# Exp issued a step later than its top-k, its reciprocal two; feed-forward pieces counted out, some held back

## The chip, the cores and the metric

One core of a Trainium2 chip runs the whole program. It has a matrix engine (TensorE, PE in the rows; PEld is its weight load), a vector engine (VectorE, DVE), an activation engine (ScalarE, ACT), a general engine (GpSimd, POOL) and a queue that starts transfers (SyncE, SP). Each engine takes its instructions in the order in which the program lists them; where one waits for another engine's result, everything behind it on its engine waits too. The metric is the device time in microseconds (us), lower is better.

## What is computed

The first half is attention in which every query keeps only its 32 largest scores. q, k and v have 8 batches, 8 heads, 576 rows and 64 columns, all in fp32:

```
scores = (q @ k.T) / 8
kth    = 32nd largest score of each row
attn   = exp(scores - max) where scores >= kth, else 0
attn   = attn / (sum(attn) + 1e-9);  x = attn @ v
```

The heads of a row are laid side by side, which gives x with 4608 rows of 512. The second half is a feed-forward layer on x, with w_in of 512 x 2048 and w_out of 2048 x 512: h = x @ w_in, g = h * clip(h + 3, 0, 6) / 6, out = g @ w_out.

## The kernel before

The program is written out as one list of steps, and the order in that list is the order on every engine. The unit of attention work (class Unit) is one pair of heads with 128 query rows: two rows of 576 scores per partition. 576 is 4 x 128 + 64, so each head pair has a remainder of 64 rows; both heads of a remainder go into one half-size unit, a rest unit. There are 160 units, 20 to a batch: 16 full and 4 rest. In an even batch four full units (the four head pairs of one query tile) are followed by a rest unit, in an odd batch the rest unit comes first.

What a unit goes through, with the lines that issue it:

- scores (L198 to L220): matmuls into big, then ScalarE copies into sc. big is one PSUM tile of four banks with a single buffer; scores, the transposes of a unit and the transposes of a pair (L171) all use it in turn, so each must wait until ScalarE has copied out the one before.
- top(0) to top(3) (L228): per row a MAX8 (eight largest) and, but for the last round, a MATCH_REPLACE8 that takes them out. All on VectorE.
- exp (L240): three tiny GpSimd operations (kth L247, shift L248 and L249), then on ScalarE two Prelu (L251) and two Exp with a sum (L256), then den on GpSimd (L261).
- weights (L263): reciprocal on VectorE (L265) and two GpSimd multiplications (L267).
- transpose (L271): nine (rest: six) transposes on TensorE into big, copied by ScalarE to eT (L280).
- values (L282): matmuls of eT with v into pv, copied to xT (L410). Full units do this two at a time, after the second of the two.

When the four head pairs of a tile are done, a feed-forward is put on the list todo; there are 36 in all. It is a generator (feed_forward, L300) that yields 16 times, so it is handed out as 16 pieces: eight h pieces of eight matmuls each, then eight acc pieces of two matmuls each. After every second h piece comes a Relu on ScalarE (L317); the multiplication that closes the gate (L321, VectorE) is called two pieces later. piece(count) takes the next pieces from the front of todo, or nothing if it is empty.

The loop from L440 runs 162 steps. Step n issues top(0) to top(3) of unit n, scores of unit n + 1, and (from step 9 on) transposes and values of unit n - 2. In the first eight steps the weights of the feed-forward are also loaded and converted (convert_step, on ScalarE, VectorE and GpSimd), and the lag is one step.

Order in a step from 9 on: scores(n + 1); top(0); two pieces (one in a rest step); top(1); transpose(n - 2); top(2); one piece; weights(n - 1); transposes of the next batch's pair, in 4 of 20 steps; one more piece in a full step; values(n - 2); top(3); two pieces more in every fourth step; exp(n). After the loop the pieces that remain run alone.

Of the kernel before, what the change touches and what calls it, by code (L numbers as in the profile page):

```python
# [27 lines left out]
def kernel(  # L28
# [17 lines left out]
    NFC = FF // P  # L46
# [140 lines left out]
    class Unit:  # L187
# [94 lines left out]
        def values(self, dst):  # L282
            pr, eT = self.pair, self.eT
            for c in range(J + 1):
                for hh in range(2):
                    if self.rest:
                        rhs = eT[:, c if c < J else J + hh, hh * R : (hh + 1) * R]
                    else:
                        rhs = eT[:, c if hh == 0 or c == J else J + 1 + c, :]
                    nc.tensor.matmul(  # L290
                        dst[hh * D : (hh + 1) * D, :],
                        pr.vm[:, hh, c, :] if c < J else pr.vr[:, hh, :],
                        rhs,
                        start=(c == 0),
                        stop=(c == J),
                    )
# [3 lines left out]
    def feed_forward(xT, rows):  # L300

        gs = []
        for f0 in range(0, NFC, 4):
            h = ps_w.tile([P, 512], F32, tag="w", name="h")
            for f in range(f0, f0 + 4):
                if f == f0 + 2:
                    yield None
                for i in range(NHP):
                    nc.tensor.matmul(  # L309
                        h[:, (f - f0) * P : (f - f0 + 1) * P],  # L310
                        w_in[:, i, f * P : (f + 1) * P],
                        xT[:, i, :],
                        start=(i == 0),
                        stop=(i == NHP - 1),
                    )
            g = gpool.tile([P, 512], F32, tag="g", name="g")
            nc.scalar.activation(g[:], h[:], AF.Relu, bias=three[:], scale=1.0)  # L317
            gs.append(g)

            def gate(g=g, h=h):  # L320
                nc.vector.scalar_tensor_tensor(  # L321
                    out=g[:], in0=g[:], scalar=6.0, in1=h[:], op0=ALU.min, op1=ALU.mult
                )

            yield gate
        acc = ps_w.tile([P, DM], F32, tag="w", name="acc")
        for f in range(NFC):
            nc.tensor.matmul(  # L328
                acc[:],
                gs[f // 4][:, (f % 4) * P : (f % 4 + 1) * P],  # L330
                w_out[:, f, :],
                start=(f == 0),
                stop=(f == NFC - 1),
            )
            if f % 2 == 1:
                if f == NFC - 1:
                    o = opool.tile([P, DM], F32, tag="o", name="o")
                    nc.scalar.mul(o[:], acc[:], 1.0 / 6.0)  # L338
                    for p0, p1, dst in rows:
                        nc.sync.dma_start(dst, o[p0:p1, :])  # L340
                yield None
# [6 lines left out]
    units = []  # L348
    for b in range(B):
        for qt in range(J):  # L350
            full = [Unit(pairs[b, hp], qt) for hp in range(NHP)]
# [4 lines left out]
    NU = len(units)  # L356
    todo = []
    gates = []

    def piece(count=1):  # L360
        for _ in range(count):
            while todo:
                try:
                    gates.append(next(todo[0]))
                    break
                except StopIteration:
                    todo.pop(0)
            else:
                gates.append(None)
            if len(gates) > 2:  # L370
                gate = gates.pop(0)
                if gate:
                    gate()
# [4 lines left out]
    def convert_step(depth=1):  # L378

        if converting and (len(converting) > depth or not chunks):  # L380
            next(converting.pop(0), None)
        if chunks:
            c = convert(*chunks.pop(0))
            next(c)
            converting.append(c)

    EARLY = 8
    LAG = 2
    state = {}

    def values(n):

        u = units[n]
        b, hp = u.pair.b, u.pair.hp
        if u.rest:
            if b % 2 == 0 and hp == 0:
                state["xr"] = xrpool.tile([P, NHP, P], F32, tag="xr", name="xr")
            group, w = [u], R
            dst = state["xr"][:, hp : hp + 1, (b % 2) * R : (b % 2 + 1) * R]
        else:  # L400
            if hp % 2 == 0:
                return
            if hp == 1:
                state["xT"] = xtpool.tile([P, NHP, P], F32, tag="xT", name="xT")
            group, w = [units[n - 1], u], P
            dst = state["xT"][:, hp - 1 : hp + 1, :]
        pv = ps_w.tile([P, 512], F32, tag="w", name="pv")
        for i, v in reversed(list(enumerate(group))):
            v.values(pv[:, i * w : (i + 1) * w])
        nc.scalar.copy(dst, pv[:, 0 : len(group) * w].rearrange("p (u q) -> p u q", q=w))  # L410
        if hp == NHP - 1:
            if not u.rest:
                rows = [(0, P, out[b * S + u.qt : b * S + JP : J, :])]
                todo.append(feed_forward(state["xT"], rows))
            elif b % 2 == 1:
                rows = [
                    (i * R, (i + 1) * R, out[(b - 1 + i) * S + JP : (b + i) * S, :])
                    for i in range(2)
                ]
                todo.append(feed_forward(state["xr"], rows))  # L420

    def pair_at(n, first):

        b, at = divmod(n, per_batch)
        hp, odd = divmod(at - first, 3)
        return pairs[b + 1, hp] if b + 1 < B and not odd and 0 <= hp < NHP else None
# [13 lines left out]
    for n in range(NU + LAG):  # L440
        early = n < EARLY
        u = units[n] if n < NU else None
        full = not (u and u.rest)
        d = n - (1 if early else LAG)
        d = d if 0 <= d < NU and (early or d >= EARLY - 1) else None
        depth = 2 if n < 3 else 1
        if n + 1 < NU:
            units[n + 1].scores()
        if n < 2:
            pairs[0, n + 2].transpose()  # L450
        if n == 0:
            pairs[0, 3].load()
        if n in (1, 2):
            pairs[0, n + 1].load_values()
        if u:
            u.begin()
            u.top(0)
        p = pair_at(n, 6)
        if p:
            p.load()  # L460
            p.load_values()
        convert_step(depth)
        piece(2 if full else 1)
        if u:
            u.top(1)
        if d is not None:
            if not early:
                units[d].transpose()
        convert_step(depth)
        if u:  # L470
            u.top(2)
        piece()
        convert_step(depth)
        if 1 <= n < NU + 1:
            units[n - 1].weights()
        if d is not None and early:
            units[d].transpose()
            piece()
        p = pair_at(n, 8)
        if p:  # L480
            p.transpose()
        if full and not early:
            piece()
        if d is not None:
            values(d)
        if u:
            u.top(3)
        convert_step(depth)
        if n % 4 == 3 and n > 2 * EARLY:
            piece(2)  # L490
        if u:
            u.exp()
    while todo:
        piece()
    piece(2)
# [34 lines left out]
```

## Time and profile before

| | |
|---|---|
| median of 3 runs | 1875.74 us (1875.71 to 1878.25) |
| the profiled execution | 1877.58 us, its span 1875.8 us |
| PE busy | 1672.3 us, 89% of the span |
| PEld busy | 1228.7 us, 66% |
| DVE busy | 1550.3 us, 83% |
| ACT busy | 964.2 us, 51% |
| POOL busy | 409.0 us, 22% |
| mean granted TensorE clock | 0.951 |

The span goes from the first to the last instruction. Busy shares are averages over stretches with different limits, and a busy PE counts its slow stretches (half clock) as busy too. The rows below come from four views: busy times by stretch, waits, the chain that ended last, and the timeline. In a timeline row the first number is the start, the second the duration of the whole group (the ends of matmuls are modelled, so the start of the next PE row is the better end), and brackets hold idle time before it and what ended it.

### The profile page before, as it was taken

To read this page: it belongs to the slowest core of one execution; us is meant where nothing else is said; L and a number is where in the kernel's file an instruction comes from. 1 tells how busy PE (TensorE), PEld (TensorE's weight loads), DVE (VectorE), ACT (ScalarE), POOL (GpSimd) and SP (SyncE) were. 2 spreads that over 40 slices of the span, in tenths; PEclk is the share of its full clock that TensorE was granted. 3 is DMA by queue.
4 is the path that set the end of the run, shared out by engine and by line. 5 is a ranking of instruction groups with operands and counts; after the bars stand their busy time and mean duration, and the time that the engine had idled before them with its cause. 6 is when DMAs were issued, how large, how long until landed. Compare 5 with 4: busy or idle time off the path is not lost.

```text
span 1875.8 us, 30943 instructions
## 1 busy us (share of the span) xinstructions
PE 1672.3 (89%) x11872; PEld 1228.7 (66%) x11872; DVE 1550.3 (83%) x3249; ACT 964.2 (51%) x1717; POOL 409.0 (22%) x1038
## 2 busy tenths in 40 slices
PE   3366999888999999889999999898899999988899
PEld 2254776666777766567777766676776767666685
DVE  6877998889988887988989888887998887888950
ACT  4554555545545554555545545545555555445540
POOL 3553221122121111221112111211211121112210
PEclk9878999899999999899999999989999999989999
DMA  6441000110010100100001110101001110000000
GB/s 188 141 125 44 20 7 7 44 45 6 7 26 26 45 7 7 44 25 20 7 9 45 27 28 7 34 11 44 7 7 26 26 44 7 6 7 6 7 7 12
DMA packets 101140, 56.53 MB, mean 30 GB/s; under 512 B 84096, under 2 KB 92288, under 8 KB 100992
## 3 DMA queue, kind: packets, MB, share of 16 engines
q1 hardware_dynamic: 100992, 54.55, 10.6%
q8 instruction: 94, 1.54, 0.3%
q14 instruction: 54, 0.44, 0.1%
HBM read 45.09 MB, written 9.44 MB: 29 GB/s over the span
## 4 chain that ended last, share of the span: by engine, by line
PE 82%; ACT 10%; issue 3%; POOL 3%; DVE 1%; SPq 1%; DMA 1%; ACTq 0%
PE h L309 27%; PE acc L328 25%; PE pv L290 11%; PE big L278 9%; PE big L214 6%; ACT sc L256 3%; ACT eT L280 2%; ACT sc L251 2%; PE big L207 2%; PE big L179 2%; ACT sc L215 1%; POOL a L108 1%; POOL w_in L121 1%; ACT o L338 1%; POOL w_out L121 1%
## 5 line engine op out<-in xcount | busy, mean ns | idle before, releaser
L231 DVE MAX8 m<-wk 128x8 f32<-128x576 f32 x864 | 614.1, 748 | 2.1
L328 PE MATMUL acc<-w_out,g 128*128 128x512 f32 x1152 | 527.8, 600 | 0.3 <-DVE g L321 0.3
L309 PE MATMUL h<-xT,w_in 128*128 128x128 f32 x4096 | 490.9, 278 | 7.4 <-DVE y L117 7.4
L309 PEld LDWEIGHTS h<-xT,w_in 128*128 128x128 f32 x4096 | 470.4, 192 | 14.0 <-DVE y L117 7.8
L235 DVE MATCH_REPLACE8 wk<-m,wk 128x576 f32<-128x576 f32 x576 | 424.0, 743 | 0.0
L328 PEld LDWEIGHTS acc<-w_out,g 128*128 128x128 f32 x1152 | 207.3, 190 | 210.1 <-issue 202.4
L278 PE MATMUL big<-ident,sc 128*128 128x128 f32 x1344 | 189.8, 289 | 122.5 <-ACT sc L218 49.2
L267 POOL TENSOR_SCALAR sc<-sc,den 128x576 f32<-128x576 f32 x288 | 212.5, 747 | 368.3 <-DVE den L265 362.9
L278 PEld LDWEIGHTS big<-ident,sc 128*128 128x128 f32 x1344 | 163.2, 150 | 163.5 <-POOL den L261 78.4
L280 ACT COPY eT<-big 128x1152 f32<-128x1152 f32 (+1 forms) x160 | 169.1, 1057 | 183.3 <-PE big L278 183.3
L251 ACT ACTIVATE sc<-sc,kth 128x576 f32<-128x576 f32 x288 | 208.7, 769 | 34.3 <-POOL kth L247 34.3
L261 POOL TENSOR_SCALAR den<-den 128x2 f32<-128x2 f32 (+1 forms) x160 | 34.9, 218 | 868.1 <-ACT sc L256 868.1
L321 DVE SCALAR_TENSOR_TENSOR g<-g,h 128x512 f32<-128x512 f32 x144 | 97.7, 679 | 151.8 <-ACT g L317 151.8
L256 ACT ACTIVATE sc<-sc,shift 128x576 f32<-128x576 f32 x288 | 219.4, 763 | 3.3 <-ACT sc L251 0.4
L317 ACT ACTIVATE g<-h,three 128x512 f32<-128x512 f32 x144 | 99.0, 687 | 229.0 <-PE h L309 229.0
L231 DVE MAX8 m<-sc 128x8 f32<-128x576 f32 x288 | 204.0, 745 | 14.8 <-ACT sc L218 14.8
L235 DVE MATCH_REPLACE8 wk<-m,sc 128x576 f32<-128x576 f32 x288 | 212.0, 743 | 0.0
L290 PE MATMUL pv<-eT,vm 128*64 128x128 f32 (+1 forms) x2560 | 188.6, 298 | 25.4 <-ACT eT L280 25.4
L290 PEld LDWEIGHTS pv<-eT,vm 128*64 128x64 f32 x2560 | 157.1, 156 | 62.9 <-ACT eT L280 32.0
L214 PE MATMUL big<-kq 64*128 64x512 f32 (+1 forms) x1024 | 179.8, 472 | 20.1 <-ACT kq L185 11.7
L214 PEld LDWEIGHTS big<-kq 64*128 64x128 f32 x1024 | 94.5, 200 | 123.7 <-issue 87.9
L410 ACT COPY xT<-pv 128x256 f32<-128x256 f32 x64 | 23.8, 373 | 232.5 <-PE pv L290 232.5
(43 smaller groups left out, 1033.9 us busy)
## 6 DMA issues: line engine op xcount, KB each, us to landing
kin<-in_k_dram SPq DMA_DIRECT2D x64, 128.0 KB, 3.1
qin<-in_q_dram SPq DMA_DIRECT2D x64, 128.0 KB, 2.9
st<-in_moe_w_in_dram SPq DMA_DIRECT2D x16, 512.0 KB, 4.1
vm<-in_v_dram SPq DMA_DIRECT2D x64, 128.0 KB, 2.4
st<-in_moe_w_out_dram SPq DMA_DIRECT2D x16, 512.0 KB, 3.7
out_dram<-o SPq DMA_DIRECT2D x32, 256.0 KB, 2.2
rest<-in_k_dram SPq DMA_DIRECT2D x32, 32.0 KB, 2.6
rest<-in_q_dram SPq DMA_DIRECT2D x32, 32.0 KB, 2.7
```

The costliest lines, as they stand in the source:

```text
L214: nc.tensor.matmul(banks[:, 2 * i + hh, 0 : s1 - s0], pr.qT[d, qs], pr.kT[d, s0:s1])
L231: nc.vector.max(self.m[:, t, 8 * r : 8 * r + 8], self.cur[t])
L235: nc.vector.match_replace(wk, self.m[:, t, 8 * r : 8 * r + 8], self.cur[t], LOWEST)
L251: nc.scalar.activation(self.row[t], self.row[t], AF.Prelu, bias=kth[:, t : t + 1], scale=1.0, alpha=STEEP,)
L256: nc.scalar.activation(self.row[t], self.row[t], AF.Exp, bias=shift[:, t : t + 1], scale=scale, accum_out=self.den[:, t : t + 1],)
L267: nc.gpsimd.tensor_scalar(self.row[t], self.row[t], self.den[:, t : t + 1], 1.0, ALU.mult, ALU.mult)
L278: nc.tensor.transpose(ps[:, i * P : (i + 1) * P], self.sc[:, c0 : c0 + P], ident[:])
L280: nc.scalar.copy(eT[:, 0:n, :].rearrange("p c q -> p (c q)"), ps[:, 0 : n * P])
L290: nc.tensor.matmul(dst[hh * D : (hh + 1) * D, :], pr.vm[:, hh, c, :] if c < J else pr.vr[:, hh, :], rhs, start=(c == 0), stop=(c == J),)
L309: nc.tensor.matmul(h[:, (f - f0) * P : (f - f0 + 1) * P], w_in[:, i, f * P : (f + 1) * P], xT[:, i, :], start=(i == 0), stop=(i == NHP - 1),)
L317: nc.scalar.activation(g[:], h[:], AF.Relu, bias=three[:], scale=1.0)
L328: nc.tensor.matmul(acc[:], gs[f // 4][:, (f % 4) * P : (f % 4 + 1) * P], w_out[:, f, :], start=(f == 0), stop=(f == NFC - 1),)
```

## The change

The counter left is the number of pieces that are on todo. At the top of a step it decides how many pieces the step hands out: with 8 or more left, two and two in a full step, one and one in a rest step; with fewer, two and one, or one and none. The extra two in every fourth step are gone.

exp(n) moves from the end of step n to step n + 1, behind top(0), the first pieces and one convert_step, and ahead of top(1). weights(n - 1) in step n becomes weights(n - 2), right behind top(0). The transposes and values keep their steps and places; in the first eight steps weights keep theirs too.

```diff
+    def queue(xT, rows):
+        nonlocal left
+        todo.append(feed_forward(xT, rows))
+        left += NFC
...
-        full = not (u and u.rest)
         d = n - (1 if early else LAG)
-        d = d if 0 <= d < NU and (early or d >= EARLY - 1) else None
+        d = units[d] if 0 <= d < NU and (early or d >= EARLY - 1) else None
...
+        if u and u.rest:
+            count = (1, 1) if left >= NFC // 2 else (1, 0)
+        else:
+            count = (2, 2) if left >= NFC // 2 else (2, 1)
...
             u.top(0)
+        if d and not early:
+            d.weights()
...
         convert_step(depth)
-        piece(2 if full else 1)
+        piece(count[0])
+        if 1 <= n < NU + 1:
+            units[n - 1].exp()
         if u:
             u.top(1)
-        if d is not None:
-            if not early:
-                units[d].transpose()
+        if d and not early:
+            d.transpose()
...
-        piece()
         convert_step(depth)
-        if 1 <= n < NU + 1:
-            units[n - 1].weights()
-        if d is not None and early:
-            units[d].transpose()
+        if d and early:
+            d.weights()
+            d.transpose()
+        if count[1]:
             piece()
...
-        if full and not early:
-            piece()
-        if d is not None:
-            values(d)
+        piece(count[1] - 1)
+        if d:
+            values(n - (1 if early else LAG))
         if u:
             u.top(3)
         convert_step(depth)
-        if n % 4 == 3 and n > 2 * EARLY:
-            piece(2)
-        if u:
-            u.exp()
```

piece also counts left down by one for each piece that it takes, and the two places that put a feed-forward on todo call queue.

## Rows read from the trace of the kernel before

**Rows 1.** Busy time by stretch: length, busy us of each engine, granted clock.

```profile
176.00:459.00 283.00, 253.21 (x1828) 186.89 (x1830) 249.92 (x528) 152.15 (x272) 58.47 (x163) 0.93 0.11 27
459.00:669.00 210.00, 204.79 (x1507) 152.64 (x1504) 185.28 (x391) 112.60 (x201) 41.73 (x116) 0.99 0.09 23
761.00:800.00 39.00, 30.84 (x217) 22.16 (x216) 35.81 (x76) 20.31 (x36) 9.36 (x27) 0.87 0.21 53
459.00:1876.00 1417.00, 1332.01 (x9555) 979.32 (x9551) 1170.69 (x2465) 721.55 (x1285) 267.92 (x744) 0.96 0.07 19
1830.00:1872.00 42.00, 42.00 (x197) 26.58 (x195) 3.44 (x5) 4.04 (x6) 0.00 (x0) 1.00 0.03 7
```

**Rows 2.** Waits of DVE, 459 to 1804: us in total, times, longest.

```profile
DVE den L265 <- POOL den L261: 91.7, 36, 6.2
DVE g L321 <- ACT g L317: 83.9, 40, 7.4
```

**Rows 3.** Waits of PE in the same stretch.

```profile
PE big L278 <- ACT sc L218: 33.3, 15, 3.2
PE pv L290 <- ACT eT L280: 16.9, 14, 1.2
```

**Rows 4.** Chain that ended last, its end: start, us, what.

```profile
1819.82 0.98 PE big L278 x9
...
1824.37 2.33 PE pv L290 x40
...
1830.47 13.74 PE acc L328 x32
1844.21 14.29 PE h L309 x128
```

**Rows 5.** Timeline, two steps with pieces in each: start, us, instruction.

```profile
911.04 0.69 PE L290 MATMUL pv<-eT,vm 128*64 128x64 f32 x16
...
911.77 1.30 PE L214 MATMUL big<-kq 64*128 64x512 f32 x8
...
912.99 3.84 PE L309 MATMUL h<-xT,w_in 128*128 128x128 f32 x32
...
916.67 1.15 PE L278 MATMUL big<-ident,sc 128*128 128x128 f32 x9
916.87 0.69 ACT L317 ACTIVATE g<-h,three 128x512 f32<-128x512 f32 x1 [0.86 <-PE h L309]
...
917.85 1.12 ACT L280 COPY eT<-big 128x1152 f32<-128x1152 f32 x1 [0.29 <-PE big L278]
918.02 0.16 DVE L265 RECIPROCAL den<-den 128x2 f32<-128x2 f32 x1
...
918.35 1.47 POOL L267 TENSOR_SCALAR sc<-sc,den 128x576 f32<-128x576 f32 x2 [3.10 <-DVE den L265]
...
922.01 1.43 ACT L251 ACTIVATE sc<-sc,kth 128x576 f32<-128x576 f32 x2
...
924.86 0.99 ACT L215 COPY sc<-big 128x1024 f32<-128x1024 f32 x1
...
925.75 0.26 ACT L218 COPY sc<-big 128x128 f32<-128x128 f32 x1
```

**Rows 6.** Timeline, scores of a rest unit and scores at half clock.

```profile
765.07 1.19 PE L207 MATMUL big<-kq 64*64 64x512 f32 x8
...
781.30 2.40 PE L214 MATMUL big<-kq 64*128 64x512 f32 x8 [1.21 <-ACT eT L280]
```

**Rows 7.** Timeline of one early step, in which weights are converted.

```profile
88.11 1.12 ACT L280 COPY eT<-big 128x1152 f32<-128x1152 f32 x1 [5.59 <-PE big L278]
...
89.13 0.67 ACT L107 ACTIVATE a<-st 128x512 f32<-128x512 f32 x1
...
91.08 1.44 ACT L251 ACTIVATE sc<-sc,kth 128x576 f32<-128x576 f32 x2 [0.75 <-POOL kth L247]
...
94.38 0.17 DVE L265 RECIPROCAL den<-den 128x2 f32<-128x2 f32 x1 [2.81 <-POOL den L261]
```

More of the change, by code (lines that the diff above doesn't have):

```diff
@@ L358 @@
     gates = []
+    left = 0
     def piece(count=1):
+        nonlocal left
         for _ in range(count):
@@ L364, in piece @@
                     gates.append(next(todo[0]))
+                    left -= 1
                     break
@@ L389 @@
     state = {}
+    def queue(xT, rows):
+        nonlocal left
+        todo.append(feed_forward(xT, rows))
+        left += NFC
     def values(n):
@@ L413, in values @@
                 rows = [(0, P, out[b * S + u.qt : b * S + JP : J, :])]
-                todo.append(feed_forward(state["xT"], rows))
+                queue(state["xT"], rows)
             elif b % 2 == 1:
@@ L419, in values @@
                 ]
-                todo.append(feed_forward(state["xr"], rows))
+                queue(state["xr"], rows)
     def pair_at(n, first):
```

## The prediction
> **What bounds the kernel now.** I first read the table of busy shares: TensorE 89%, VectorE 83%, neither full, so the stretches decide. I cut the span at 459 us, where step 37 begins on VectorE: up to there the start-up and the first batch and a half run, from there the same pattern of 40 steps repeats. From 459 to the end TensorE is busy 1332.0 of 1417 us, and at a granted clock of 0.96 [rows 1]. So 85 us of idle time, and 0.04 x 1417 = 57 us in which a clock at its lower level (1.2 instead of 2.4 GHz) made work longer; the rounding allows 50 to 64, I take 54. VectorE is busy 1170.7 us in it.
>
> The two short rows show why. From 459 to 669 there are always pieces on the list, and TensorE is busy 204.8 of 210 us at clock 0.99. From 761 to 800 (steps 64 to 66, where by counting the calls of piece through the code only two pieces are handed out) it is busy 30.8 of 39 us at 0.87 [rows 1]. In the 123 steps from 37 to 159 that count gives 22 full steps with six pieces, 65 with four and 12 with two or none, while six of the 24 rest steps have none. Steps with six overfill TensorE, and VectorE then stands at its two waiting points: 91.7 us at the reciprocal, which waits for Exp and den, and 83.9 us at the gate, which waits for a Relu behind the matmuls [rows 2]. Steps with none starve TensorE, which then waits for copies of scores that stand on ScalarE behind exp (33.3 us), and for eT (16.9 us) [rows 3].
>
> Is TensorE the bound? The Trainium skill (Perfetto Trace Analysis, Identifying the Most-Contended Engine) says that matmul busy time is a bad measure of the room left, because matmuls are pipelined, and that the busy share of weight loads is the better one: 979.3 of 1417 us, 69%, would leave a third free. By it VectorE would bind, with a time as in rival D below. The trace differs: from 1830 to 1872 TensorE runs alone and never waits, and its weight loads are busy 26.6 of 42 us, 63% [rows 1]. With this mix 63 to 70% is full. I follow the rows.
>
> **The pieces, as a sum over TensorE.** I rebuild the time from 459 us on as work at full clock plus idle time. One feed-forward alone takes 14.29 + 13.75 us (the acc row shown has 13.74) [rows 4]: 28.04 / 16 = 1.753 us a piece. Scores of a full unit: 911.77 to the next row at 912.99, 1.22 us [rows 5]; of a rest unit 1.19 less the 0.1 by which modelled ends overlap, 1.1 [rows 6]. Nine transposes 0.98, so six 0.65; values of two full units 2.33, 1.165 each [rows 4]; of a rest unit 911.04 to 911.77, 0.73 [rows 5]; a pair's nine transposes 0.98 like the others.
>
> At step 37 both kernels have 16 pieces on the list and seven feed-forwards queued, so 576 - 96 = 480 pieces are left: 841.2 us. Scores of units 38 to 159: 98 x 1.22 + 24 x 1.1 = 146.0. Transposes of units 35 to 159: 100 x 0.98 + 25 x 0.65 = 114.3. Their values: 100 x 1.165 + 25 x 0.73 = 134.8. 25 pairs: 24.5. Together 1260.8 us. TensorE takes up step 37 about 4 us after VectorE, at 463.1, and behind the last matmul stand 3.5 us of copy and store: 463.1 + 1260.8 + 3.5 = 1727.4. The span is 1875.8, so 148 us lie between. Idle time within is 85 - 3.5 = 81.5, the clock 54; 12 us are gaps too small for the waits, which I leave as they are.
>
> The change hands out, by the same count, four pieces in 96 of 99 full steps and two in 23 of 24 rest steps; only four steps hand out less. A full step then costs TensorE 1.22 + 0.98 + 1.165 + 4 x 1.753 = 10.4 us. VectorE needs in it 1170.7 / (99 + 12) = 10.5 us, if a rest step counts half. So both are level there, but TensorE also has the pieces behind the loop: 32 are left instead of 26, six more or 10.5 us. That lengthens the tail and shortens the loop by as much, since the pieces are the same ones; it is in the sum. VectorE's own end would be 459 + 1170.7 = 1630 us, then 32 + 8 pieces and some 5 us of transposes and values, 75 us: 1705, under 1727. TensorE stays the bound, by little.
>
> **What the order costs.** exp(n - 1) now stands on ScalarE behind the copies of scores(n + 1) and in front of the eT copy of unit n - 2. It no longer holds the score copies, which removes the first wait of [rows 3], and Exp and den have most of a step until the reciprocal, which removes the first wait of [rows 2]. New is a wait of TensorE for eT: big has one buffer, so the next user of big, and values, queue behind that copy. The two Prelu and two Exp take 922.01 to 924.86 = 2.85 us, score copies 0.99 + 0.26, Relu 0.69, eT copy 1.12 [rows 5]. Counted from the start of the scores on TensorE:
>
> - Full step in which a Relu stands ahead of exp (33 steps): matmuls and two pieces end at 4.8, Relu from 5.1 to 5.8, exp to 8.6, eT to 9.8. TensorE wants it at 4.8 + 0.98 + 3.5 = 9.3. It waits 0.5: 16 us.
> - The same in a step with a pair (6 steps): wanted one piece earlier, 7.5. It waits 2.2: 13 us.
> - Rest step with no Relu ahead (19): copies end at 2.8, exp at 5.6, eT at 6.7; wanted at 1.2 + 0.98 + 2 x 1.75 = 5.7. It waits 1.0: 19 us. With one (5): eT at 8.0, 2.3, so 11 us.
> - Other steps: exp ends ahead of the transposes, nothing; pairs at 0.3 x 6 = 2 us.
>
> Sum 61 us where 81.5 stood. All of this needs the weights by the transposes: reciprocal 918.02, multiplications 918.35 to 919.8 [rows 5], so 1.8 us behind top(0), at about 4.8 us of VectorE's step, and TensorE comes there at 4.8 of its own. VectorE must not lag, and it may lead, by up to some 3 us until its gate waits for Relu; the rest steps, where it has the lighter load, give it that lead. The reciprocal queues ahead of top(1); with the lead it finds den done.
>
> **The clock.** In the stretch with pieces throughout the clock was 0.99, in the starved one 0.87 [rows 1], and scores took 2.40 instead of 1.30 us at the lower level [rows 5, 6]. Without starved steps I keep 8 of the 54 us; bounds 0 and 54. The Trainium skill (TensorE: Matmul & The Clock Gate, Part 1) says that the low clock is the default and activity releases it. The trace agrees, its low stretches stand behind starved steps; by that rule all 54 would go, and the sum would be 8 lower.
>
> **Ahead of step 37.** From 176 to 459 VectorE is busy 249.9 of 283 us [rows 1], so at most 33 us can go; production of pieces still limits TensorE there (six rest steps with one piece, six full ones with less than four). I take half: -15. In the first eight steps exp now stands behind the score copies and one conversion on ScalarE. In the row of before, eT ends at 89.23, Abs starts 89.13, Prelu 91.08, reciprocal 94.38, VectorE having waited 2.81 for it [rows 7]; with scores (2.40 at half clock), copies and two conversions between, but with GpSimd no longer held by den in front of its conversions, the loop of 15.3 us grows by about 1 us a step: +7, bounds -5 and +20. Net -8.
>
> **Sum.** 1727.4 - 8 + 12 + 61 + 8 = 1800.4 us span. The profiled execution lies 1.8 us above its span, so 1802.2; it is itself 1.8 us, 0.1%, above the median, within what is told as no change here (0.2%). Forecast 1802 us, 76 under 1877.6, 4% faster.
>
> **Rivals.**
> A, slower. The eT copy behind exp hits every step, not 63 of them, because VectorE gets no lead: with weights late, exp late too (kth queues on GpSimd behind the multiplications). For: full steps are level within 0.1 us between the two engines; ScalarE is one queue. Against: ScalarE is half empty, rest steps give room. It decides where the mean wait over 123 steps passes (61 + 75) / 123 = 1.1 us; at 1.3 us a step, 160 us, the time is 1901. Chance 0.11.
> B, the low clock stays, 54 instead of 8 us: 1848, still faster. For: rest steps keep a gap; against: 0.99 where pieces were never short. Chance 0.12.
> C, no change: the counted pieces do even things out, but waits of about 1.05 us a step eat it: 1873 to 1881. Chance 0.04.
> D, VectorE binds, as the page's rule would have it: 1705 plus what TensorE can't hide, or simply fewer waits than I count: 1705 to 1762. For: 20 to 30 us of my sum are waits that may be absorbed. Against: 63% alone. Chance 0.07.
> The forecast itself, 1762 to 1835, has 0.66.
>
> **Chances and range.** Faster by over 0.2%: 0.66 + 0.12 + 0.07 = 0.85; within: 0.04; slower: 0.11. Range 1765 to 1855: it takes in B, and leaves out A, C and most of D.
>
> **What would show it.** Right: waits of VectorE for den and for Relu fall from 176 us to under 60; TensorE's wait for copies of scores goes and its wait for eT grows to 40 to 80 us, most of it in rest steps and steps with a pair; no stretch behind 459 us with the clock under 0.95; the last 56 us are pieces alone. Wrong: transposes waiting for the GpSimd weights in most steps (A), a clock that still falls twice a batch (B), or TensorE idle for over 1 us in every step.

## The result, and the profile after

The changed kernel takes 1806.38 us (median of 4 runs, 1803.79 to 1808.42) against 1876.88 us, a ratio of 0.9623 with a 95% interval of 0.9607 to 0.964: 70 us or 3.8% faster. Forecast were 1802 us, and 1765 to 1855 as the range. The profiled execution has 1803.79 us and a span of 1802.0.

Busy time of the changed kernel by stretch (columns as in [rows 1]). Step 37 begins on VectorE at 461.2 us, so its long stretch goes from 461:

```profile
176.00:459.00 283.00, 253.38 (x1837) 183.25 (x1836) 252.56 (x534) 158.44 (x284) 59.97 (x168) 0.95 0.10 24
459.00:669.00 210.00, 203.01 (x1540) 151.14 (x1539) 192.20 (x406) 116.68 (x207) 42.85 (x119) 1.00 0.09 24
761.00:800.00 39.00, 37.14 (x260) 26.18 (x257) 35.23 (x75) 18.72 (x34) 7.67 (x23) 1.00 0.21 52
461.00:1802.00 1341.00, 1302.76 (x9570) 954.38 (x9568) 1170.33 (x2466) 726.43 (x1287) 267.63 (x745) 0.99 0.08 20
1745.00:1798.00 53.00, 53.00 (x293) 37.34 (x291) 5.50 (x8) 6.10 (x9) 0.00 (x0) 1.00 0.02 6
```

Against [rows 1]: the stretch that was starved (761 to 800) is now as full as any, 37.1 of 39 us at clock 1.00 instead of 30.8 at 0.87. From step 37 to the end TensorE's idle time fell from 85 us (1417 - 1332.0) to 38 (1341 - 1302.8), its busy time from 1332 to 1303, with the clock at 0.99 instead of 0.96. Ahead of 176 us nothing was won, and between 176 and 459 next to nothing. The last row is the tail of pieces alone.

Waits of VectorE from 461 us to its last MAX8, then waits of TensorE from 459 to 1745 us, both of the changed kernel (columns as in [rows 2]):

```profile
DVE g L321 <- ACT g L317: 53.8, 42, 3.0
DVE den L265 <- POOL den L261: 18.9, 20, 3.4
DVE m L231 <- ACT sc L218: 14.5, 11, 2.3
DVE m L231 <- ACT sc L209: 5.9, 3, 3.7
```

```profile
PE big L214 <- ACT eT L280: 14.8, 16, 2.2
PE big L179 <- ACT eT L280: 13.1, 11, 1.9
PE pv L290 <- ACT eT L280: 0.9, 3, 0.4
```

Both waits of [rows 2] shrank, 91.7 to 18.9 and 83.9 to 53.8 us; 20 us of waits for score copies are new. Of [rows 3] the wait for score copies is gone; TensorE now waits for eT, 29 us in 30 times. That looks just like the prediction. The experiments show that its account of what brought this about was half wrong.

### The profile page after: what moved, and what is told of

Same layout as the page of the kernel before. It is cut to its first block, busy times and chain, and to the rows that moved or that the text cites. A ratio compares the mean times of both kernels' runs of the same rounds, so it can differ in the third digit from the quotient of the medians.

```text
span 1802.0 us, 31081 instructions
## 1 busy us (share of the span) xinstructions
PE 1638.0 (91%) x11872; PEld 1198.3 (66%) x11872; DVE 1548.2 (86%) x3249; ACT 968.7 (54%) x1717; POOL 408.3 (23%) x1038
## 4 chain that ended last, share of the span: by engine, by line
PE 68%; ACT 15%; DVE 9%; issue 5%; POOL 2%; DMA 1%; SPq 0%; ACTq 0%
PE acc L328 22%; PE h L309 20%; PE pv L290 9%; PE big L214 8%; ACT sc L256 6%; DVE m L231 5%; PE big L278 5%; ACT eT L280 4%; DVE wk L235 4%; ACT sc L251 3%; PE big L179 2%; PE big L207 1%; DVE g L321 1%; DMA st<-in_moe_w_in_dram 1%; POOL a L108 1%
## 5 line engine op out<-in xcount | busy, mean ns | idle before, releaser
L328 PE MATMUL acc<-w_out,g 128*128 128x512 f32 x1152 | 540.6, 608 | 0.3 <-DVE g L321 0.3
L278 PE MATMUL big<-ident,sc 128*128 128x128 f32 x1344 | 181.0, 281 | 70.3 <-POOL sc L267 69.0
L215 ACT COPY sc<-big 128x1024 f32<-128x1024 f32 x128 | 129.6, 1013 | 136.6 <-PE big L214 136.6
L290 PE MATMUL pv<-eT,vm 128*64 128x128 f32 (+1 forms) x2560 | 163.9, 272 | 9.6 <-ACT eT L280 8.5
L290 PEld LDWEIGHTS pv<-eT,vm 128*64 128x64 f32 x2560 | 134.8, 140 | 52.4 <-issue 27.6
```

Of the source, the lines that this page charges most:

```text
L215: nc.scalar.copy(sc[:].rearrange("p (h s) -> p h s", h=2)[:, :, 0:JP], banks[:, 0:2, 0:JP])
L278: nc.tensor.transpose(ps[:, i * P : (i + 1) * P], self.sc[:, c0 : c0 + P], ident[:])
L290: nc.tensor.matmul(dst[hh * D : (hh + 1) * D, :], pr.vm[:, hh, c, :] if c < J else pr.vr[:, hh, :], rhs, start=(c == 0), stop=(c == J),)
L328: nc.tensor.matmul(acc[:], gs[f // 4][:, (f % 4) * P : (f % 4 + 1) * P], w_out[:, f, :], start=(f == 0), stop=(f == NFC - 1),)
```

## Experiments: which part does it

First the two parts of the change apart. Where nothing else is said, an edit is shown against the changed kernel. Counted pieces alone, exp and weights where they were (the piece that stands beside the weights goes back with them):

```diff
-        if d and not early:
-            d.weights()
...
-        if 1 <= n < NU + 1:
-            units[n - 1].exp()
...
+        if 1 <= n < NU + 1:
+            units[n - 1].weights()
...
+        if u:
+            u.exp()
```

> The counted handing-out of pieces alone; exp and the weights stay where they were before. Theory (TensorE is the bound and what it loses is starved steps and low clock): most of the 71 us comes from here, since in the stretch of before that was never short of pieces TensorE was already busy 204.8 of 210 us with the old order. 1805 to 1830 us, granted clock 0.965 or more. Rival (the places of exp and weights do it): 1855 to 1880 us.

Measured: 1768.43 us, ratio to before 0.9423 (0.9403 to 0.9443). It is faster than everything expected, and 38 us faster than the whole change. Its stretch from step 37 on, and TensorE's largest wait in it:

```profile
442.00:1769.00 1327.00, 1292.93 (x9556) 948.93 (x9555) 1168.66 (x2464) 721.25 (x1286) 268.49 (x744) 1.00 0.08 21
```

```profile
PE big L278 <- POOL den L261: 22.7, 18, 1.3
```

With exp in its old place, ahead of the score copies on ScalarE, the 33.3 us wait for these copies [rows 3] is nevertheless gone, and no other took its size: when pieces are even, TensorE has work until the copies come. TensorE's idle time from step 37 on is 34 us (1327 - 1292.9) instead of 85, its busy time 1293 instead of 1332, the clock 1.00. VectorE's waits up to its last MAX8 are about half of [rows 2]:

```profile
DVE den L265 <- POOL den L261: 44.2, 23, 3.9
DVE g L321 <- ACT g L317: 37.2, 40, 2.9
```

The other half alone:

```diff
-        if u and u.rest:
-            count = (1, 1) if left >= NFC // 2 else (1, 0)
-        else:
-            count = (2, 2) if left >= NFC // 2 else (2, 1)
+        count = (1, 1) if u and u.rest else (2, 2)
...
+        if n % 4 == 3 and n > 2 * EARLY:
+            piece(2)
```

> The new places of exp and weights with the old handing-out (two, one, one, and two more in every fourth step). Theory: steps with six pieces and with none stay, so the clock stays at about 0.95 and the time at 1850 to 1880 us; the waits of VectorE for den fall, those for Relu stay. Rival (the places do it): 1800 to 1825 us.

Measured: 1900.39 us, 1.0122 (1.0101 to 1.0142), slower than before. The new places are a loss by themselves, which no case of the prediction had beside a gain in all. TensorE's waits from step 37 on:

```profile
PE big L179 <- ACT eT L280: 27.4, 18, 1.9
PE pv L290 <- ACT eT L280: 24.9, 16, 3.5
PE big L278 <- ACT sc L218: 18.6, 14, 1.3
```

The score copies are waited for less than before (18.6 instead of 33.3 us), but 52 us of waiting for eT in the first two rows are new in this size. VectorE's wait for den, on the other hand, falls as far as in the changed kernel:

```profile
DVE den L265 <- POOL den L261: 18.1, 22, 2.6
```

So the change is two parts of opposite sign: with counted pieces, the places cost 1806 - 1768 = 38 us; without them, 25. These waits are not all of it. Much of either cost has gathered by the first MAX8 of step 37, in this kernel (before: 459.2 us) and with counted pieces alone (changed kernel: 461.2 us):

```profile
476.24 0.74 DVE L231 MAX8 m<-sc 128x8 f32<-128x576 f32 x1
```

```profile
441.73 0.75 DVE L231 MAX8 m<-sc 128x8 f32<-128x576 f32 x1
```

That is 17 of the 25 us, and some 19 of the 38 (33 between the two profiled spans).

Does the counting matter, or holding some back? Once in the new order, once in the old one, every step hands out two and two, in rest steps one and one, whatever is left:

```diff
-        if u and u.rest:
-            count = (1, 1) if left >= NFC // 2 else (1, 0)
-        else:
-            count = (2, 2) if left >= NFC // 2 else (2, 1)
+        count = (1, 1) if u and u.rest else (2, 2)
```

> As the changed kernel, but always two and two (one and one in a rest step), also with fewer than eight left. From step 37 on only four steps hand out less in the changed kernel, so theory puts the difference ahead of step 37, where steps with no piece come back: 5 to 15 us slower than the changed kernel, 1811 to 1821 us. Rival (holding back is what evens the load): 1835 us or more. Second rival: no difference, 1803 to 1809.

> Counted pieces alone had 1768 us; here nothing is held back (always two and two, one and one in a rest step), exp and weights in their old places. In the new order, holding back cost 11 us, most of it as low clock. If that is general: 1755 to 1762 us. If it comes from the new order (where a piece stands against a Relu ahead of exp): 1764 to 1774 us. If holding back evens the load as it was told: 1780 us or more.

Measured: 1794.98 us in the new order (0.957, 0.9544 to 0.9597), 11 us faster than with the reserve, so I had the sign wrong; 1771.46 us in the old one (0.9427, 0.9396 to 0.9459), 3 us slower, with an interval that covers the 0.9423 of counted pieces alone. The reserve is no gain. The second of these kernels also differs from the kernel before in nothing but the two lines that gave two pieces more in every fourth step: it issues the same instructions in the same order but for these. Taking out those two lines is worth 104 us against the 1875.79 us of before that stands beside counted pieces alone, 112 against the 1883.16 us beside its own runs. From step 37 on they filled 22 steps with six pieces and so left 12 full ones with two or none.

## Experiments: what the new places cost

The places apart, both with counted pieces and shown against counted pieces alone; in the first only exp is moved, in the second only the weights:

```diff
         piece(count[0])
+        if 1 <= n < NU + 1:
+            units[n - 1].exp()
...
-        if u:
-            u.exp()
```

> Counted pieces as in the changed kernel; exp in its new place (behind the first pieces, ahead of top(1) and of the transposes), the reciprocal and the GpSimd multiplications in their old one. Theory now: what the order costs is that the copy to eT stands behind exp on ScalarE, so this is as slow as the changed kernel, 1795 to 1815 us. Rival (the weights' place right behind top(0) costs it): 1763 to 1775 us, as with counted pieces alone.

```diff
             u.top(0)
+        if d and not early:
+            d.weights()
...
-        if 1 <= n < NU + 1:
-            units[n - 1].weights()
         if d and early:
+            d.weights()
```

> Counted pieces; exp in its old place at the end of the step, the weights in their new one, right behind top(0) of the step that transposes them. Theory: no cost, 1763 to 1773 us against 1768 with counted pieces alone. Rival (weights come too late for the transposes): 1785 us or more, with waits of TensorE for the GpSimd multiplications above 60 us in all.

Measured: 1796.24 us (0.9556, 0.9529 to 0.9584) and 1792.13 us (0.9544, 0.9513 to 0.9575). The first was expected, and its waits for eT from step 37 on are those of the changed kernel, 14.8 and 13.1 us for scores and pairs. The second hit its rival: the weights' place costs 24 us by itself. TensorE's largest wait from step 37 on in the second one is for the multiplications, where the kernel with counted pieces alone has no such row:

```profile
PE big L278 <- POOL sc L267: 30.6, 25, 1.6
```

The two costs, 28 and 24 us (25 and 23 by the ratios), don't add up to some 50 but to the 38 of both together: beside exp's new place, the weights' place, with a piece of the first eight steps that the change moves too (below), costs another 10 (1806 - 1796).

Now the wait for eT at its root. From step 9 on exp is issued behind the transposes, so that on ScalarE the eT copy comes first:

```diff
-        if 1 <= n < NU + 1:
+        if 1 <= n < NU + 1 and early:
             units[n - 1].exp()
         if u:
             u.top(1)
         if d and not early:
             d.transpose()
+        if 1 <= n < NU + 1 and not early:
+            units[n - 1].exp()
```

> As the changed kernel, but from step 9 on exp(n - 1) is issued behind the transposes of unit n - 2, so that on ScalarE the copy to eT stands ahead of the two Prelu and two Exp. Theory (TensorE waits for eT behind exp, 29 us from step 37 on in the changed kernel): these waits fall under 8 us and the time to 1775 to 1793 us. Rival (VectorE paces, TensorE's waits are absorbed): 1800 to 1810. Second rival (exp now so late that Relu and den come late): over 1812, with the waits of VectorE at the gate above 80 us.

Measured: 1763.02 us (0.9392, 0.9371 to 0.9413), 43 us faster than the changed kernel and more than expected. From step 37 on:

```profile
453.00:1761.00 1308.00, 1289.25 (x9515) 948.89 (x9511) 1166.06 (x2465) 722.04 (x1285) 266.37 (x745) 1.00 0.08 21
```

Step 37 comes 8 us earlier than in the changed kernel; the stretch behind it is 33 us shorter, of which 19 are idle time (38 to 19) and 14 busy time. The same place in both, step 131 with a pair; first the changed kernel, then this one (start, us, instruction):

```profile
1436.25 0.82 PE L278 MATMUL big<-ident,sc 128*128 128x128 f32 x6
1436.45 0.69 ACT L317 ACTIVATE g<-h,three 128x512 f32<-128x512 f32 x1 [2.58 <-PE h L309]
1436.90 1.95 PE L309 MATMUL h<-xT,w_in 128*128 128x128 f32 x16
1437.04 1.43 ACT L251 ACTIVATE sc<-sc,kth 128x576 f32<-128x576 f32 x2
...
1439.89 0.78 ACT L280 COPY eT<-big 128x768 f32<-128x768 f32 x1
...
1440.72 0.66 PE L179 MATMUL big<-ident,kin 128*128 128x128 f32 x4 [1.86 <-ACT eT L280]
```

```profile
1399.73 0.82 PE L278 MATMUL big<-ident,sc 128*128 128x128 f32 x6
1399.93 0.69 ACT L317 ACTIVATE g<-h,three 128x512 f32<-128x512 f32 x1 [2.58 <-PE h L309]
1400.38 1.95 PE L309 MATMUL h<-xT,w_in 128*128 128x128 f32 x16
1400.58 0.80 ACT L280 COPY eT<-big 128x768 f32<-128x768 f32 x1
1401.28 1.45 ACT L251 ACTIVATE sc<-sc,kth 128x576 f32<-128x576 f32 x2
...
1402.17 0.60 PE L179 MATMUL big<-ident,kin 128*128 128x128 f32 x4
```

In both the transposes are followed by one piece, and then the pair's transposes want big. In the upper one Relu and 2.85 us of Prelu and Exp stand ahead of the eT copy, and 4.47 us lie between the two uses of big; in the lower one the copy follows Relu at once, 2.44 us, the length of transposes and piece. TensorE's waits from step 37 on in the lower kernel:

```profile
PE big L214 <- ACT kq L185: 7.8, 3, 2.9
PE big L207 <- ACT kq L185: 3.8, 5, 1.1
PE big L278 <- POOL sc L267: 1.9, 3, 0.8
PE big L214 <- ACT eT L280: 1.2, 1, 1.2
```

The 29 us for eT are 1.2, and the largest wait left is 7.8, for kq. The weights stay in their new place here, and the 30.6 us wait for them that the kernel with only the weights moved had is 1.9. So exp's place decides what the weights' place costs; whether their old place would be better still beside exp behind the transposes, no run shows.

## Experiments: the bound, and the start

Which engine binds? In the changed kernel, once two of the 16 acc matmuls of each feed-forward are left out, once the third MATCH_REPLACE8 of the second row of each full unit:

```diff
-            nc.tensor.matmul(
+            if f < NFC - 2:
+                nc.tensor.matmul(
...
-                stop=(f == NFC - 1),
+                    stop=(f == NFC - 3),
```

> The changed kernel with the last two of the 16 acc matmuls of every feed-forward left out (output columns lack two chunks of the hidden layer); pieces are still 16. That takes 36 x 2 x 0.43 = 31 us off TensorE and nothing off VectorE. If TensorE is the bound from step 37 on: 1775 to 1785 us, against 1806. If VectorE or the waits between the two set the pace, less than a third: 1796 us or more.

```diff
             if r < TOP_K // 8 - 1:
-                for t in range(self.nt):
+                for t in range(1 if r == 2 else self.nt):
```

> The changed kernel with the third MATCH_REPLACE8 left out for the second row of each full unit (the threshold of that row is then another one). That takes 128 x 0.82 = 105 us off VectorE (of 1548) and nothing off TensorE. If TensorE is the bound from step 37 on, only the steps ahead of it (30 units, 25 us) and part of the lead that VectorE then has come back: 1770 to 1795 us. If VectorE is the bound: 1700 to 1730 us.

Measured: 1753.23 us (0.9317, 0.9289 to 0.9344) and 1801.82 us (0.9581, 0.9551 to 0.9611). The first expectation counted one record of 0.43 us for each matmul; there are two, as the page of this run shows with 11728 instructions on TensorE, 144 less than 11872 for 72 matmuls. So 62 us went from TensorE and the time fell by 53. Less work on VectorE gave 5 us: 1801.82 lies outside both expected ranges, 7 us above the one for a bound on TensorE and 72 above the one for VectorE. The long stretch of this second kernel:

```profile
460.00:1798.00 1338.00, 1299.64 (x9571) 952.36 (x9569) 1105.06 (x2268) 726.80 (x1287) 267.62 (x745) 1.00 0.08 20
```

VectorE is 65 us less busy in it than in the changed kernel (1170.3), and the stretch is 3 us shorter. TensorE is the bound, clearly. Its weight loads are busy 954 of 1341 us in the changed kernel from step 37 on, 71%. The Trainium skill (Perfetto Trace Analysis, Identifying the Most-Contended Engine) names this share as one of two measures of TensorE's headroom; taken alone it would leave 29%. These two runs show no such room. Step 37 began at 459.9 us in the run with less work on VectorE, 1.3 earlier: ahead of step 37 VectorE doesn't bind either.

The start was 8 us longer in the changed kernel: step 9, with its first MAX8, begins at 175.5 us, before at 167.6. I had put that down to exp. Exp behind the transposes from step 9 on, and in the first eight steps at the end of the step as before:

```diff
-        if 1 <= n < NU + 1:
-            units[n - 1].exp()
...
+        if EARLY < n < NU + 1:
+            units[n - 1].exp()
...
+        if early and u:
+            u.exp()
```

> The changed kernel with exp behind the transposes from step 9 on (1763 us), and in the first eight steps exp at the end of the step as before. Theory: the start-up loop loses its extra, step 9 starts at 168 to 170 us instead of 174.5, and the time is 1754 to 1759 us. Rival (the loss at the start is absorbed later, since TensorE is short of pieces up to step 37): 1762 to 1766 us.

Measured: 1761.03 us (0.937, 0.9342 to 0.9397), no better than its parent within what these runs tell, and step 9 still at 173.8. The diff holds one more move, which I had passed over: in the first eight steps the third piece went from ahead of the weights and transposes to behind them. Taken back, shown against the kernel just told of:

```diff
             u.top(2)
+        if early and count[1]:
+            piece()
...
-        if count[1]:
+        if count[1] and not early:
             piece()
```

> As the kernel with exp behind the transposes and exp at the end of the step in the first eight (1761 us; step 9 starts at 173.8 us), and now the third piece of those eight steps is again issued ahead of the weights and transposes, as it was before the change. The change had moved it behind them, which the prediction did not price. If that move is what makes the start-up longer: step 9 at 167 to 170 us and 1754 to 1758 us. If not: step 9 at 173 to 175 and 1759 to 1763 us.

Measured: 1748.88 us (0.9305, 0.9283 to 0.9328), more than expected and the fastest of all. The first MAX8 of step 9 in the changed kernel, with exp back, and with the piece back too:

```profile
175.48 0.76 DVE L231 MAX8 m<-sc 128x8 f32<-128x576 f32 x1 [1.53 <-ACT sc L209]
```

```profile
173.84 0.76 DVE L231 MAX8 m<-sc 128x8 f32<-128x576 f32 x1 [3.18 <-ACT sc L209]
```

```profile
166.77 0.76 DVE L231 MAX8 m<-sc 128x8 f32<-128x576 f32 x1 [1.66 <-ACT sc L209]
```

With exp back, the piece is worth 7 of the 8 us; of the 12 us between the last two kernels 9 show by step 37 (449.9 and 440.8 us). But exp's new place does the same harm alone. Step 9 with counted pieces alone, and with only exp moved, the piece in its old place in both:

```profile
170.05 0.74 DVE L231 MAX8 m<-sc 128x8 f32<-128x576 f32 x1
```

```profile
176.50 0.74 DVE L231 MAX8 m<-sc 128x8 f32<-128x576 f32 x1
```

So either move makes the start some 7 us longer, and both together (175.5) no more than one. One more kernel is the one of 1761 us, exp at the end of the step in the first eight and behind the transposes later, without the reserve (the same lines as above):

> Exp behind the transposes from step 9 on, exp at the end of the step in the first eight (1761 us), and nothing held back. In the changed kernel, holding back cost 11 us, by low clock; with the old order it gave 3. Without the waits for eT there is little left for it to do: 1754 to 1764 us. If holding back costs in the new order in any case: 1745 to 1753 us.

Measured: 1759.44 us (0.9358, 0.9333 to 0.9384). With no waits for eT the reserve makes no difference that these runs can tell.

## Why the prediction was right, step by step

- *TensorE is the bound, and its work at full clock is a floor of 1727 us.* The bound is right: 53 of 62 us came back on the one side, 5 of some 84 on the other (VectorE's busy time in the whole span fell from 1548.2 to 1464.0). The work was sized too small. In the fastest kernel, from step 37 on TensorE to its last matmul, at clock 1.00, TensorE is busy 1288 us, 27 more than the 1260.8 of the sum, which had left 12 for small gaps:

```profile
440.65:1743.80 1303.15, 1288.13 (x9517) 947.90 (x9515) 1166.44 (x2466) 721.74 (x1284) 266.38 (x745) 1.00 0.08 21
```

- *Even pieces remove starved steps and low clock.* Right, and larger than I made it: alone it is worth 107 us. The clock from step 37 on is 0.99, as forecast.
- *The order removes the first waits of [rows 2, 3].* This step failed in what it was to be worth. With even pieces and the old order the wait for score copies is gone as well; the order removed what was no longer there. The wait for den it does cut, 91.7 to 18.1 us by itself, where even pieces leave 44.2, but that is a wait of VectorE, which isn't the bound: the order alone made the kernel slower. The sum came out because I had priced the order's new waits and let the old ones go, whichever part removed them.
- *TensorE waits 61 us for eT.* Right in kind, half in size: 29 us in the view. The 2.2 us in steps with a pair were 1.9. The 0.5 us in 33 full steps don't appear as waits, and of the 30 us that I gave to rest steps, after which scores want big, the view has 14.8 in 16 waits. Taking the cause away gave 43 us, though, more than the waits: 8 lie ahead of step 37, and of the 33 behind it 14 are busy time, with the clock at 1.00 instead of 0.99. How much of the 14 is the clock, and how much are small gaps that the modelled ends of matmuls hide, these runs don't settle.
- *Ahead of step 37, 8 us less.* It was 2 more (461.2 instead of 459.2). The +7 at the start was right in size (8 measured), and exp's place alone does cost it; the moved piece, which I hadn't priced, would have cost it too. The -15 between 176 us and step 37 was the mis-sized term: from step 9 to step 37 the time fell from 291.6 to 285.7 us, so 6. I took VectorE's idle time as what can be won there; with some 19 us less work on VectorE ahead of step 37 (84 in all, 65 behind it), step 37 came only 1.3 us earlier. With even pieces in the old order it was 271.7 (170.1 to 441.7), 20 less than before, so the 15 were there, and the new order spent them: with only exp moved it was 284.3 (176.5 to 460.8).
- *Sum.* The errors offset each other: from step 37 to the end 1349 us were forecast and 1341 measured, ahead of it 451 and 461. From step 37 on TensorE to its last matmul, in the changed kernel:

```profile
466.52:1798.00 1331.48, 1297.24 (x9517) 950.55 (x9515) 1164.81 (x2453) 724.10 (x1284) 266.29 (x741) 0.99 0.08 20
```

  TensorE took up step 37 at 466.5 instead of 455.1 us (463.1 - 8), 11 later; it was then idle 34 instead of 61 us, 27 less, and busy 1297 instead of 1281 (1260.8 + 12 + 8), 16 more. That these three cancel to within 2 us is luck; the bound, the clock and the sign were not.
- *Signs.* VectorE's waits for den and Relu were to fall under 60 us; they are 73, from 176. The clock and the tail came as forecast.
- *Rivals.* A was right about the queue, wrong about how often it bites. B, C and D are out. That a part of the change is a loss was the case of none of them: the total alone could not have told.

## What to carry to other kernels

When a change has two parts, run each alone even if the total comes out as forecast: here -107 and +38 us hid behind a correct -70. Even out the filler work of the bound engine before moving any wait: waits seen beside uneven filler may vanish with it. When an instruction group moves on an in-order queue, look first at what it now stands ahead of, and whether that releases a single buffer; here one copy of 1.1 us behind 2.9 us of exp cost 43 us of 1806. And a move may cost nothing beside another one and something by itself, so each is taken back alone too: at the start of this kernel either of two moves cost some 7 us, and both no more.

## What the runs showed of the hardware

Each fp32 matmul of the program is two records on TensorE: 72 fewer matmuls of 128 x 512 are 144 fewer records, and 0.86 us each by the 0.43 us spacing of the acc rows (13.74 us for 32 records in [rows 4]). The clock granted from step 37 on was 0.96 before, 0.97 with the new order and uneven pieces, and 0.99 to 1.00 in every kernel with even pieces. The Trainium skill (TensorE: Matmul & The Clock Gate, Part 1) calls the low clock the default that activity releases; these rows agree.
